# Three chained layers on one core: issue order written out for all engines, and seven products for the second product of two passes

## The chip, the cores and the metric

The kernel runs on one core of one Trainium2 chip. The metric is device time in microseconds, as the median of several executions. The engines that matter are PE (TensorE, matrix products), DVE (VectorE), ACT (ScalarE), POOL (GpSimd) and SP, whose queue issues the DMA transfers.

## The reference

Four batches of attention between 512 tokens and 32 state vectors (8 heads of 64) give 4 x (512 + 32) = 2176 rows of 512. These rows go through two layers:

```
scores = x @ state.T / 8;   xread = softmax(scores) @ state
scores2 = state @ x.T / 8;  sread = softmax(scores2) @ x
h = rows @ w_in             # 512 -> 1024
solu = h * softmax(h);  ln = (solu - mean) / sqrt(var + 1e-6) * g_ln
y = ln @ w_out              # 1024 -> 512
h = y @ w2_in               # 512 -> 2048
g = h * tanh(softplus(h))   # Mish
out = g @ w2_out            # 2048 -> 512
```

The four weight matrices arrive as 64-bit floats, all else as 32-bit.

## The kernel before

**Numbers.** A product that has to be exact to 32 bits is made of three products of shorter ones: each operand is split into a high part (a copy on ACT that rounds, `hi`) and the rest (a subtraction on DVE, `lo`), and PE adds hi*lo, hi*hi and lo*hi into one accumulator in PSUM. A 64-bit weight is first turned into 32 bits by `narrow` (lines 43 to 64): scale the high word (ACT, line 53, or DVE, line 51), shift the low word (ACT, line 55, or DVE, line 57), and either a copy of the sign to 16 bits on ACT (line 59) and one DVE operation (line 60) or two DVE operations (lines 60 and 63).

**First stage (to about 240 us).** The 2176 rows are 17 tiles of 128 rows. Attention and w_in are folded together: state @ w_in is made for each batch (`sw`, tiles swh and swl), and `stage_a0` (line 549) multiplies the softmax weights of a tile (aThi, aTlo) by it, 12 matmuls of 512 columns for each of 16 tiles, and 16 of line 555 for the tile of state rows. `stage_a1` to `stage_a3` (lines 564 to 588) make the softmax and the norm on DVE and ACT; `stage_c` and `stage_e` turn the tile, in part through DRAM (td). `stage_d` (line 645) multiplies by g*w_out in blocks of two tiles (256 columns, the last block 384), 24 matmuls for each of four parts. The result stays in SBUF, features on the partitions (raw_a, raw_c, raw_d).

**Second stage (from about 240 us).** The 17 tiles go in three passes of 6, 6 and 5 tiles; each pass runs over 8 groups (`fp`) of 256 of the 2048 features. In a group the first product (`hp`, line 787, in `group`) is done as a 2 x 2 block product by seven products instead of eight (Strassen's method in Winograd's form); the seven products have 6 matmuls each, of 384 columns in passes 0 and 1 and 320 in pass 2. Seven DVE additions (line 808) and a copy (line 823) put the blocks together, ACT makes Mish of each block twice (lines 817 and 818), once rounded to `gh`, and DVE subtracts for `gl` (line 819). The second product (`po`, `out_parts`, lines 768 to 770) then takes 3 matmuls of 512 columns for each of 2 features blocks and each tile: 36 a group in passes 0 and 1, 30 in pass 2, into one PSUM bank for each tile.

**Weights of the second stage.** In pass 0 they are prepared group by group: `load64` loads 512 KB (tile w, three buffers), narrows it, `pieces_in` makes the four sums that the seven products need and splits seven blocks (lines 188 to 199), and writes them to DRAM (`kept`); `pieces_out` splits w2_out into w2oh and w2ol (lines 217 and 218), which stay in SBUF. Passes 1 and 2 fetch the seven blocks of w2_in again.

**Order.** The text PLAN lists the steps of the first stage, each a whole function (load, narrow, one stage of one tile), and one digit per place that says which engine takes an operation. The second stage is a fixed loop: after each of the seven products comes a part of the `po` work of the group before. A scheduler of the language may move instructions within that.

## Time and profile before

| | |
|---|---|
| median of 3 executions | 606.2 us (603.38 to 608.51) |
| span of the profiled execution | 600.7 us |
| PE busy | 571.1 us, 95% |
| DVE busy | 401.9 us, 67% |
| ACT busy | 302.5 us, 50% |
| DMA | 94.29 MB, mean 157 GB/s |

The profile comes from one execution, whose span runs from its first to its last instruction. The views used are busy time by window, the chain of work that ended last in order of time, the waits (who waited for whom), and timelines of single engines. In a timeline the distance from one start to the next on an engine that never idles is what one instruction occupies; the recorded length of an instruction can be more, since records of neighbours overlap.

### The profile page before, as it was taken

What the parts mean: (1) busy time and instruction counts of PE and PEld (TensorE: products, weight loads), DVE (VectorE), ACT (ScalarE), POOL (GpSimd) and SP (SyncE); (2) the same over time, 40 slices, a digit from 0 to 9 for tenths busy, and PEclk for the clock granted to TensorE, in tenths of its full rate; (3) what the DMA queues carried; (4) which work ended last, traced back from release to release, by engine and by line L of the source; (5) the groups of instructions that cost most, each with busy time, mean ns of one, the idle gap of its engine ahead of it and who ended that gap; (6) DMA issues with size and microseconds to landing.
All of it is one profiled execution on the core that took longest, in us unless ns stands there. A gap on an engine that the chain in (4) does not pass through costs nothing.

```text
span 600.7 us, 8857 instructions
## 1 busy us (share of the span) xinstructions
PE 571.1 (95%) x3371; PEld 491.2 (82%) x3371; DVE 401.9 (67%) x739; ACT 302.5 (50%) x572; POOL 33.4 (6%) x102
## 2 busy tenths in 40 slices
PE   8487899899999999999999999999999999999997
PEld 4145488599799999899989899999999989989885
DVE  3999986898969987878888986333333553443332
ACT  2796866665645644656664765222222452332323
POOL 0002221022111100000000000000000000000000
PEclk9786999899999999999999999999999999999999
DMA  8931321622525645833763575323232354244402
GB/s 321 415 131 35 106 71 52 206 97 71 193 72 172 207 151 195 317 113 144 278 245 117 175 271 210 141 106 140 106 140 106 141 198 153 105 167 163 161 1 88
DMA packets 31050, 94.29 MB, mean 157 GB/s; under 512 B 3616, under 2 KB 11424, under 8 KB 30496
## 3 DMA queue, kind: packets, MB, share of 16 engines
q1 hardware_dynamic: 31008, 93.73, 43.8%
q8 instruction: 26, 0.43, 0.3%
q14 instruction: 16, 0.13, 0.1%
HBM read 69.87 MB, written 23.86 MB: 156 GB/s over the span
## 4 chain that ended last, share of the span: by engine, by line
PE 75%; DVE 13%; DMA 5%; ACT 4%; issue 2%; SPq 1%; ACTq 0%; DVEq 0%
PE hp L787 23%; PE pm L645 16%; PE po L768 8%; PE po L769 8%; PE po L770 8%; PE ph L549 7%; DMA w<-in_w2o 3%; PE ph L555 1%; DVE w L60 1%; DMA xT_t<-in_xT 1%; DVE gw_lo L530 1%; PE tr L603 1%; DMA w<-in_w2i 1%; ACT w L59 1%; DVE wo L60 1%
## 5 line engine op out<-in xcount | busy, mean ns | idle before, releaser
L817 ACT ACTIVATE gh<-c 128x384 fp32r<-128x384 f32 (+1 forms) x96 | 48.9, 509 | 157.5 <-DVE c L808 156.4
L768 PE MATMUL po<-w2ol,gh 128*128 128x512 f32 x272 | 106.8, 393 | 0.1
L769 PE MATMUL po<-w2oh,gh 128*128 128x512 f32 x272 | 106.5, 392 | 0.0
L787 PE MATMUL hp<-xo,w2r 128*128 128x384 f32 (+1 forms) x504 | 93.6, 329 | 0.0
L787 PEld LDWEIGHTS hp<-xo,w2r 128*128 128x128 f32 x504 | 86.5, 188 | 4.8
L787 PE MATMUL hp<-xo,w2swh 128*128 128x384 f32 (+1 forms) x336 | 82.9, 330 | 2.4 <-DVE c L808 2.0
L770 PE MATMUL po<-w2oh,gl 128*128 128x512 f32 x272 | 82.1, 391 | 0.0
L645 PE MATMUL pm<-ln_lo,gw_hi 128*128 128x256 f32 (+1 forms) x256 | 75.3, 294 | 0.0
L645 PE MATMUL pm<-ln_hi,gw_hi 128*128 128x256 f32 (+1 forms) x256 | 75.0, 293 | 0.0
L645 PE MATMUL pm<-ln_hi,gw_lo 128*128 128x256 f32 (+1 forms) x256 | 74.5, 291 | 0.0
L787 PEld LDWEIGHTS hp<-xo,w2swh 128*128 128x128 f32 x336 | 60.5, 188 | 8.3 <-DVE c L808 2.6
L768 PEld LDWEIGHTS po<-w2ol,gh 128*128 128x128 f32 x272 | 51.1, 188 | 9.3 <-ACT gh L817 0.8
L769 PEld LDWEIGHTS po<-w2oh,gh 128*128 128x128 f32 x272 | 51.1, 188 | 8.2
L770 PEld LDWEIGHTS po<-w2oh,gl 128*128 128x128 f32 x272 | 50.1, 188 | 7.7
L787 PE MATMUL hp<-xo,w2swl 128*128 128x384 f32 (+1 forms) x168 | 55.1, 329 | 0.0
L808 DVE TENSOR_TENSOR c<-hp,u 128x384 f32<-128x384 f32 (+1 forms) x48 | 25.6, 534 | 42.7 <-PE hp L787 42.7
L808 DVE TENSOR_TENSOR c<-hp,m 128x384 f32<-128x384 f32 (+1 forms) x48 | 25.6, 532 | 37.3 <-PE hp L787 37.2
L645 PEld LDWEIGHTS pm<-ln_lo,gw_hi 128*128 128x128 f32 x256 | 48.2, 188 | 0.7 <-ACT e L427 0.2
L645 PEld LDWEIGHTS pm<-ln_hi,gw_lo 128*128 128x128 f32 x256 | 48.7, 190 | 0.1
L645 PEld LDWEIGHTS pm<-ln_hi,gw_hi 128*128 128x128 f32 x256 | 48.2, 188 | 0.2
L787 PEld LDWEIGHTS hp<-xo,w2swl 128*128 128x128 f32 x168 | 31.5, 188 | 0.0
L808 DVE TENSOR_TENSOR u<-hp,u 128x384 f32<-128x384 f32 (+1 forms) x24 | 12.8, 535 | 24.7 <-PE hp L787 24.7
(365 smaller groups left out, 907.4 us busy)
## 6 DMA issues: line engine op xcount, KB each, us to landing
w<-in_w2i SPq DMA_DIRECT2D x16, 512.0 KB, 6.5
w<-in_w2o SPq DMA_DIRECT2D x16, 512.0 KB, 4.0
td<-tt SPq DMA_DIRECT2D x9, 512.0 KB, 2.8
ln_lo<-td SPq DMA_DIRECT2D x36, 128.0 KB, 2.9
wi<-in_w_in SPq DMA_DIRECT2D x8, 512.0 KB, 9.1
xT_t<-in_xT SPq DMA_DIRECT2D x16, 256.0 KB, 4.5
wo<-in_w_out SPq DMA_DIRECT2D x4, 1024.0 KB, 11.8
xn_t<-in_xn SPq DMA_DIRECT2D x16, 256.0 KB, 3.8
```

The lines of the kernel that those rows point to most:

```text
L59: nc.scalar.copy(out=src.bitcast(F16)[..., 1], in_=f32(high))
L60: nc.vector.scalar_tensor_tensor(out=words(dst) if sign_on_scalar else low, in0=high, scalar=3, in1=low, op0=ALU.logical_shift_left, op1=A ...
L530: nc.vector.scalar_tensor_tensor(out=gw_lo[sl], in0=wr[:, k, :], scalar=g_k, in1=f32(gw_hi[sl]), op0=ALU.mult, op1=ALU.subtract)
L549: nc.tensor.matmul(out=ph[:, hf * 512:(hf + 1) * 512], lhsT=a_[:, c * P:(c + 1) * P], rhs=w_[:, q, hf * 512:(hf + 1) * 512], start=n == 0, ...
L555: nc.tensor.matmul(out=ph[:, hf * 512:(hf + 1) * 512], lhsT=tl["xs"][:, p, :], rhs=w_in_half[2 * p + hf], start=p == 0, stop=p == 3)
L645: nc.tensor.matmul(out=pm[:, :n], lhsT=w_[:, k, m * P:(m + 1) * P], rhs=l_[:, c0:c0 + 4 * len(blk), k, :], start=cnt == 0, stop=cnt == 23)
L768: nc.tensor.matmul(out=po[ps, j], lhsT=gh[:, c], rhs=wl, start=first, stop=False)
L769: nc.tensor.matmul(out=po[ps, j], lhsT=gh[:, c], rhs=wh, start=False, stop=False)
L770: nc.tensor.matmul(out=po[ps, j], lhsT=gl[:, c], rhs=wh, start=False, stop=f == NF - 1)
L787: nc.tensor.matmul(out=r, lhsT=w_[:, 0, k * P:(k + 1) * P], rhs=x_[:, k, :n], start=cnt == 0, stop=cnt == 6 * len(terms) - 1)
L808: nc.vector.tensor_tensor(out=r, in0=y, in1=x, op=ALU.add)
L817: nc.scalar.activation(out=gh, in_=src, func=AF.Mish)
```

## The change

**Order.** PLAN goes. Every step of both stages is now a generator that issues a few instructions and stops, and ORDER lists 3142 turns of 1019 steps, two letters a turn. Under `manual_schedule` all engines and SP get their instructions in just this order. FLAGS again says which engine takes which operation; the sign copy on ACT (T) is taken at 18 of 28 places, where it was at 4.

**Room layout.** The even and odd batches swap rooms, loads of w2_out have rooms of their own (`s_load64`), and the first loads are three of the four parts of w_out.

**First batch first, in the order of tiles.** Ahead of the first `s_d` (the new `stage_d`) stand all of batch 0's `s_a0` (four tiles), the narrowing of w_in and w_out, and no tile of the other batches.

**Seven products for the second product.** In passes 1 and 2 the weights stand still and the activations move, so the result has features on the partitions, and it is written so (the host puts the rows back). It is a 2 x 2 block product by seven products: 7 blocks x 2 parts x 3 matmuls of 384 (pass 1) or 320 columns (pass 2) a group. Its sums of activations are made in each group (`s_tsum`, `s_tsplit`); five of the seven blocks are added up in SBUF by DVE (`s_block`), two stay in PSUM. The last group of pass 2 stays plain (`s_end`, 8 parts x 6 matmuls of 320). In pass 0 the sums of w2_out are made, split and written to DRAM as well (`s_sums64`, `s_split_osum`, `s_keep_out`), and passes 1 and 2 fetch 14 blocks of 128 KB more a group (`s_fetch_out`). In the first product, sums that DVE made are now made by PE in the PSUM bank (`STEPS`, `s_hp`): five additions and a copy are left.

```diff
-PLAN = """
...
-wm,22 lb,0 lw,3,0 lb,1 lw,1,0 lx,0 lw,1,1 lo,0,1 lw,3,1 lw,0,1 wi,3,1 lw,2,1 lw,0,0 lw,2,0 wi,1,0 lo,1,1 wi,3,0
...
-        for step in PLAN.split():
+FLAGS = dict(
...
+    T="1111100010011000101111011111",
...
+ORDER = (
+    "AAAAA4A4ADA2A2A6A6ABABAEAEAwAwAGAGAkAkA5A5AuAuADA5A5AIAIA3A3BABBA3AKAKA7A3AqAqAsAsBHA7BBBEA7BAAFAFAxAmAmAxAxBEAx"
...
+    live = {}
+    with tc.manual_schedule():
+        for i in range(0, len(ORDER), 2):
+            n = 64 * CODE.index(ORDER[i]) + CODE.index(ORDER[i + 1])
+            if n not in live:
+                step, step_args = steps[n]
+                live[n] = step(*step_args)
+            next(live[n], None)
...
-            for _ in range(1 if b in (B11, T3) else 2):
-                next(more, None)
-            m1_ = temp("m1")
-            nc.scalar.copy(out=m1_, in_=step(A11, B11))
-            active(add("c0", m1_, step(A12, B21)), 0, 0)
-            next(part)()
-            u2 = add("u2", m1_, step(S2, T2))
...
+    def s_load64(which, f):
+        if which and 4 <= f < 8:
+            room = once("room", lambda: x2p.tile([P, 3, 512, 2], U32, tag="x0", name="room"))[:, f % 3]
+        elif which and f >= 8:
+            room = aTp.tile([P, 512, 2], U32, tag="aT", name="w64")
+        else:
+            room = w64_p.tile([P, 512, 2], U32, tag="w64", name="w64")
+        w64[which, f] = room
+        nc.sync.dma_start(out=room, in_=(w2i, w2o)[which][f])
+        yield
+        yield from narrow(nc, f32(room[..., 0]), room, 12 + f)
...
+    def s_split_osum(fp, j):
+        e = f32(w64[1, 2 * fp + j][..., 1]).rearrange("p (n c) -> p n c", c=256)
+        hi, lo = (out_sums(fp, d)[:, 2 * j:2 * j + 2] for d in range(2))
+        nc.scalar.copy(out=hi, in_=e)
+        yield
+        on('H', 4 * fp + 2 + j).tensor_tensor(out=lo, in0=e, in1=f32(hi), op=ALU.subtract)
...
+    def s_keep_out(fp, d, j):
+        if j == 2:
+            nc.sync.dma_start(out=kept_o[fp][:, d, 4:8], in_=f32(out_sums(fp, d)))
+        else:
+            n = 1 if j == 0 and fp < NFP - 1 else 2
+            nc.sync.dma_start(out=kept_o[fp][:, d, 2 * j:2 * j + n], in_=f32(operands(out_place(fp)[d], 2 * j, n)))
+        yield
...
+    def s_fetch_out(ps, fp, d):
+        n = (ps * NFP + fp) % 2
+        t = once(("fo", ps, fp), lambda: [rings[0].tile([P, 8, 256], F32R, tag=f"o{n}{h}", name="w2o" + h) for h in "hl"])
+        W["s", ps, fp] = t
+        if ps == NPASS - 1 and fp == NFP - 1:
+            cuts = ((0, 4),)
+        else:
+            cuts = ((0, 1), (2, 8))
...
+    STEPS = ((A11, B11), (S2, T2), (A12, B21), (S3, T3), (S1, T1), (A22, T4), (S4, B22))
+    WHICH = ((OA11, "b11"), (OA12, "b21"), (OS4, "b22"), (OS1, "t1"), (OS2, "t2"), (OS3, "t3"), (OA22, "t4"))
+    HELD = (5, 6)
...
+    def s_hp(ps, fp):
+        n = width(ps)
+        for s, (a, b) in enumerate(STEPS):
+            t = "xyxyxyx"[s]
+            fresh = s in (0, 1, 4)
+            if fresh:
+                bank[ps, fp, t] = phase2["g"].tile([P, 512], F32, tag="h" + t, name="hp")[:, :n]
+                if s == 4:
+                    bank[ps, fp, "z"] = bank[ps, fp, t]
+            r = bank[ps, fp, t]
+            bank[ps, fp, s] = r
+            x = xop[ps, b]
+            wh, wl = (operands(place, a) for place in W[ps, fp])
+            cnt = 0
+            for k in range(2):
+                for w_, x_ in ((wh, x[1]), (wh, x[0]), (wl, x[0])):
+                    nc.tensor.matmul(out=r, lhsT=w_[:, 0, k * P:(k + 1) * P], rhs=x_[:, k, :n],
+                                     start=s in (0, 1, 3, 4) and cnt == 0, stop=cnt == 5,
+                                     skip_group_check=s not in (0, 1, 3, 4))
+                    cnt += 1
+            yield
...
+        u2 = temp(ps, "u2")
+        nc.vector.tensor_tensor(out=u2, in0=bank[ps, fp, 1], in1=m1_, op=ALU.add)
+        yield
+        u3 = temp(ps, "u3")
+        nc.vector.tensor_tensor(out=u3, in0=bank[ps, fp, 3], in1=u2, op=ALU.add)
+        yield
+        for s, name, u, blk in ((4, "c2", u3, (1, 1)), (5, "c1", u2, (1, 0)), (6, "c0", u2, (0, 1))):
+            c = temp(ps, name)
+            tmp[ps, fp, blk] = c
+            nc.vector.tensor_tensor(out=c, in0=bank[ps, fp, s], in1=u, op=ALU.add)
+            yield
...
+            gh, gl = (phase2["wk"].tile([P, 384], F32R, tag=f"g{j}{half}{t}", name="g" + t, bufs=2)[:, :n] for t in "hl")
+            gs[ps, fp, j, half] = (gh, gl)
+            name = {(0, 0): "b11", (1, 0): "b21", (1, 1): "b22"}.get((j, half))
+            tq[ps, fp, name] = (gh, gl)
+            nc.scalar.activation(out=gh, in_=src, func=AF.Mish)
+            yield
+            value()
+            yield
+            on('L', (ps * NFP + fp) * 4 + 2 * j + half).tensor_tensor(out=gl, in0=vals[ps, fp, j, half], in1=f32(gh), op=ALU.subtract)
+        else:
...
+            t[name] = tsum[ps, fp, name] = phase2["t"].tile([P, 384], F32, tag=name, name=name)[:, :n]
+            y = t[y] if y in t else vals[(ps, fp) + y]
+            on('J', ((ps - 1) * NFP + fp) * 4 + int(name[1]) - 1).tensor_tensor(out=t[name], in0=vals[(ps, fp) + x], in1=y, op=ALU.subtract)
+            yield
...
+        tq[ps, fp, name] = (hi, lo)
+        nc.scalar.copy(out=hi, in_=src)
+        yield
+        on('V', ((ps - 1) * NFP + fp) * 4 + int(name[1]) - 1).tensor_tensor(out=lo, in0=src, in1=f32(hi), op=ALU.subtract)
...
+        held = i in HELD
+        tag = f"po{2 * HELD.index(i) + m}" if held else f"po{4 + m}"
+        if first or not held:
+            po[ps, i, m] = phase2["o"].tile([P, 512], F32, tag=tag, name="po")[:, :n]
+        r = po[ps, i, m]
+        c = slice(m * P, m * P + P)
+        nc.tensor.matmul(out=r, lhsT=wh[:, a, c], rhs=x[1], start=first or not held, stop=False)
+        nc.tensor.matmul(out=r, lhsT=wh[:, a, c], rhs=x[0], start=False, stop=False)
+        nc.tensor.matmul(out=r, lhsT=wl[:, a, c], rhs=x[0], start=False, stop=last or not held)
+        yield
+        side = on('E', ps - 1)
...
+            if not held:
+                add(s[i], r, s[i])
...
+            for w_, x_ in ((wh, gl), (wh, gh), (wl, gh)):
+                nc.tensor.matmul(out=r, lhsT=w_[:, a, c], rhs=x_, start=cnt == 0, stop=cnt == 5)
+                cnt += 1
```

## Rows read from the trace of the kernel before

**Rows 1.** Windows: length, busy us of PE, PEld, DVE, ACT, POOL; clock, DMA share, GB/s

```profile
0.00:84.00 84.00, 62.96 (x369) 35.81 (x369) 71.36 (x124) 56.81 (x98) 9.76 (x37) 0.86 0.49 180
84.00:240.00 156.00, 153.97 (x1192) 136.94 (x1193) 129.85 (x211) 92.44 (x161) 23.64 (x66) 0.99 0.43 142
240.00:361.00 121.00, 118.97 (x592) 107.10 (x593) 103.18 (x214) 73.95 (x144) 0.00 (x0) 1.00 0.57 207
361.00:486.00 125.00, 125.00 (x625) 113.26 (x624) 54.66 (x102) 42.04 (x88) 0.00 (x0) 1.00 0.36 131
486.00:595.00 109.00, 108.97 (x595) 97.44 (x594) 42.89 (x93) 36.08 (x85) 0.00 (x0) 1.00 0.36 132
```

**Rows 2.** The start: windows, line 645's first matmul (PE timeline), line 549 until then (window)

```profile
20.00:40.00 20.00, 11.77 (x42) 3.94 (x42) 20.00 (x32) 17.56 (x25) 0.00 (x0) 0.72 0.72 277
40.00:60.00 20.00, 15.69 (x69) 11.54 (x62) 19.48 (x38) 13.37 (x28) 3.58 (x12) 0.68 0.18 53
...
83.94 0.39 PE L645 MATMUL pm<-ln_lo,gw_hi 128*128 128x256 f32 x1
...
0.00:83.90 83.90, 21.31 (x72) 14.85 (x72) 0.86 0.49 181
```

**Rows 3.** Chain in time order: start, us, engine, tile, line, count

```profile
177.91 5.46 PE ph L549 x24
...
347.87 1.37 PE po L770 x6
...
411.13 1.06 PE hp L787 x6
...
426.78 1.06 PE hp L787 x6
...
515.46 0.88 PE hp L787 x6
```

**Rows 4.** DVE timeline, passes 0 and 2: start, us, line, operation, tiles

```profile
312.99 0.55 DVE L808 TENSOR_TENSOR c<-hp,m 128x384 f32<-128x384 f32 x1
313.46 0.69 DVE L60 SCALAR_TENSOR_TENSOR w<-w 128x512 uint32<-128x512 uint32 x1
314.06 0.56 DVE L819 TENSOR_TENSOR gl<-a__3249,gh 128x384 fp32r<-128x384 f32 x1
...
590.01 0.48 DVE L808 TENSOR_TENSOR m<-hp,u 128x320 f32<-128x320 f32 x1
590.41 0.48 DVE L819 TENSOR_TENSOR gl<-a__5792,gh 128x320 fp32r<-128x320 f32 x1
```

**Rows 5.** ACT timeline, pass 0

```profile
297.25 0.51 ACT L818 ACTIVATE a__3100<-c 128x384 f32<-128x384 f32 x1
297.67 1.34 ACT L59 CAST w<-w 128x512 f16<-128x512 f32 x1
298.76 0.73 ACT L53 ACTIVATE w<-w 128x512 f32<-128x512 f32 x1
...
303.40 1.21 ACT L198 CAST w2r<-w 128x512 fp32r<-128x512 f32 x2
```

**Rows 6.** Waits: engine, tile, line, releaser; us in total, times, longest

```profile
ACT w L55 <- DMA w<-in_w2i: 7.5, 4, 2.3
...
ACT w L55 <- DMA w<-in_w2o: 5.6, 3, 2.4
...
ACT w L53 <- DMA w<-in_w2o: 3.1, 2, 2.5
...
ACT w L53 <- DMA w<-in_w2i: 2.9, 3, 1.2
```

**Rows 7.** Last matmul and last copy, timeline of all engines

```profile
595.84 0.39 PE L770 MATMUL po<-w2oh,gl 128*128 128x512 f32 x1
...
597.02 0.59 ACT L736 COPY ob<-po 128x512 f32<-128x512 f32 x1 [0.62 <-DMA out<-ob]
```

More of the change, by code (lines that the diff above doesn't have):

```diff
@@ L1 @@
 import math
-from contextlib import ExitStack, contextmanager
-from itertools import chain
+from contextlib import ExitStack
 import concourse.bass as bass
@@ L137, in how, with once @@
-    def how(i):
-        return eng('B', i, False, True)
-    def signs(i):
-        return eng('T', i, False, True)
-    def keep_up(dst, n):
-        for _ in range(n):
-            nc.tensor.matmul(out=dst, lhsT=spare[:, :dst.shape[0]], rhs=spare.unsqueeze(1).to_broadcast([P, 4, P]),
-                             start=True, stop=True)
-    def times(i):
-        return 3 * int(flags["D"][i])
+    tl, raw = {}, {}
+    def once(key, make):
+        if key not in tl:
+            tl[key] = make()
+        return tl[key]
@@ new lines, in w_in_half, with s_warm, s_load_bd @@
+    def w_in_half(i):
+        if i == 7:
+            return once("w_in_7", lambda: m1.tile([P, 512], F32, tag="w7", name="w_in_7"))
+        return once("w_in", lambda: wx_p.tile([P, 7, 512], F32, tag="wx7", name="w_in_t"))[:, i]
+    def s_warm(n):
+        dst = ps_m.tile([P, 512], F32, tag="mm", name="warm")
+        for _ in range(n):
+            nc.tensor.matmul(out=dst, lhsT=spare, rhs=spare.unsqueeze(1).to_broadcast([P, 4, P]), start=True, stop=True)
+        yield
+    def s_load_bd(i):
+        dst, src = ((bd_t, bd), (st_t, stT))[i]
+        nc.sync.dma_start(out=dst, in_=src)
+        yield
@@ new lines, in s_tok_turn, with s_scores0 @@
+    def s_tok_turn(b, q):
+        ex = toks[b].rearrange("p (c q r) n -> p c q (r n)", c=4, q=2)
+        tr = turn4(ex[:, :, q, :]).rearrange("p c t -> p (c t)")
+        yield
+        yield from weights_of(b, q, tr)
+    def s_scores0(q):
+        sts[0, q] = st = ps_m.tile([P, S], F32, tag="mm", name="st")
+        for j in range(2):
+            p = 2 * q + j
+            nc.tensor.matmul(out=st[of_head(j), :], lhsT=bd_t[:, p, :], rhs=xT_t[0, p], start=True, stop=True)
+            yield
@@ L161, in ring, with operands, ring_in @@
+    def operands(place, i, n=1):
+        for i0, n0, t in place:
+            if i0 <= i and i + n <= i0 + n0:
+                return t[:, i - i0:i - i0 + n]
+    def ring_in(fp):
         if fp % 2 == 0:
@@ L895 @@
     r = run_bass_kernel_spmd(nc, [arrays], core_ids=[0])
-    return r.results[0]["out_0"]
+    flat = r.results[0]["out_0"]
+    y = np.empty((NTOK, DM), flat.dtype)
+    done = 0
+    for ps, places in enumerate(PASSES):
+        n = len(places) * P
+        part = flat[done * DM:(done + n) * DM]
+        part = part.reshape(n, DM) if ps == 0 else part.reshape(DM, n).T
+        done += n
+        for j, place in enumerate(places):
+            t = TILE_AT[place]
+            rows = part[j * P:(j + 1) * P]
+            if t < 16:
+                b, s = divmod(t, 4)
+                y[b * (S + NS) + s * P:][:P] = rows
+            else:
+                for b in range(B):
+                    y[b * (S + NS) + S:][:NS] = rows[b * NS:(b + 1) * NS]
+    return y
```

1400 lines of the change are left out of this document (779 added, 621 removed).

## Prediction

> **What bounds the kernel now.** I read the windows by stage first [rows 1]. Up to 84 us PE is busy 63 of 84 us at a mean clock of 0.86 of full, while DVE is busy 71. After that PE is the bound: its idle time is 2.0 us from 84 to 240, 2.0 us in pass 0 (240 to 361), and none in passes 1 and 2. So only two things can move the end: fewer or shorter matmuls after about 84 us, or an earlier time at which PE has enough to do. The windows of the start show why PE waits: from 20 to 60 us DVE is busy 39.5 of 40 us, PE 27.5, and the clock granted to PE is 0.72 and 0.68 of full, a mean over stretches at its two levels of 1.2 and 2.4 GHz [rows 2]. The first matmul of line 645 starts at 83.9 us; by then 72 of the 192 matmuls of line 549, six tiles of sixteen, are done [rows 2]. The end hangs on PE: the last matmul ends at 595.84 + 0.39 = 596.2 us, then a copy and a store take the 4.5 us to 600.7 [rows 7].
>
> The chain in time order gives PE's prices [rows 3]: six `hp` matmuls of 384 columns follow each other in 1.06 us (177 ns each), of 320 columns in 0.88 us (147 ns); six of 512 take 1.37 us (229 ns); a tile of line 549 takes 5.46 / 2 = 2.7 us. A group of pass 1 lasts 426.78 - 411.13 = 15.65 us = 42 x 0.177 + 36 x 0.229: no gap.
>
> The DVE timeline gives starts in an unbroken run [rows 4]: an operation of 384 columns begins 0.47 us before the next, one of 512 0.60, one of 320 0.40, though their records are 0.55, 0.69 and 0.48 long. On ACT [rows 5] a Mish of 384 occupies 0.42 us, the sign copy 298.76 - 297.67 = 1.09, a copy of 512 0.6.
>
> **Part 1, the second product: PE loses 11.2 us.** Pass 0 keeps 36 matmuls of 229 ns a group. Pass 1: 7 blocks x 2 parts x 3 = 42 matmuls of 384 columns, 42 x 0.177 = 7.43 us in place of 36 x 0.229 = 8.24: 0.81 x 8 groups = 6.5 us. Pass 2: 42 x 0.147 = 6.17 in place of 30 x 0.229 = 6.87: 0.70 x 7 groups = 4.9 us; the plain last group has 48 x 0.147 = 7.06, 0.2 more. Together 6.5 + 4.9 - 0.2 = 11.2 us. Shape and count of `hp` stay.
>
> What pays for it is DVE. A group of passes 1 and 2 has 5 additions after `hp`, 3 `gl`, 4 sums, 4 splits and 10 block additions, 26 where there were 11. At the distance between starts that is 26 x 0.47 = 12.2 us in a group of 7.43 + 42 x 0.177 = 14.9 us of PE (82%) in pass 1, and 26 x 0.40 = 10.4 of 12.3 us (84%) in pass 2; it was 55 of 125 and 43 of 109 us [rows 1]. ACT has 12 operations, some 5 us. I cost this work at nothing, covered by PE, but allow 2 us over both passes for places where a bank waits for DVE: five of seven blocks use only two banks, and each must be read by DVE before PE may refill it. Without cover it costs what DVE exceeds PE by (rival 2).
>
> Whether a DVE operation blocks the next for 0.47 us or for its whole record of 0.55 is what this rests on, and [rows 4] show 0.47 where nothing waited. The Trainium skill, "VectorE: DVE Perf Modes", section "The DRAIN you can't avoid", says that the next operation cannot issue until the pipe of the one before is empty, and advises fewer operations above all; it speaks against this part. Taken as the whole record, pass 2 would need 26 x 0.48 = 12.5 us of DVE for 12.3 of PE, and the end would come some 1.5 us later; the row bears out the shorter figure.
>
> **Part 2, the start: 13.6 us earlier at the first `s_d`.** In ORDER, what stands on DVE ahead of the first `s_d` is 20 operations of 1024 columns (1.13 each, going on from 0.47 and 0.60), 46 of 512 (0.60) and some 24 scalar or tiny ones (7 us, an estimate): 22.6 + 27.6 + 7 = 57 to 58 us. Before it was 71.4 [rows 1]: two tiles fewer are in work and five of the second narrowing operations of w_in and w_out have become sign copies on ACT. DVE's time not busy before 83.9 us was 83.9 - 71.3 = 12.6 us. With the same 12.6 the first `s_d` comes at 57.7 + 12.6 = 70.3. Bounds: 66.7 if only the 9 us until the first data are lost, 83.9 if nothing is gained. I take 70.3, not less, because ACT's list for the same stretch is 56 us too (it was 56.8 of 84 us), so two engines are full that wait for each other. PE's own list ahead of it is some 36 us and fits at either clock. The clock of 0.7 stays until then.
>
> What PE has not done by then: two more tiles of line 549 (4 of 16 done instead of 6), 5.5 us, and some 2 us of small products: 7.5 us.
>
> **Part 3, pass 0: 4 us lost.** Here the change adds: sums, splits and stores of w2_out. The list between the first `hp` of pass 0 and that of pass 1 has PE 117 us (56 products and 84 of the 96 x 3 `po` matmuls), DVE 111 and ACT 104. Before, DVE was busy 103 and ACT 74 of 121 us [rows 1]; ACT's 30 us more are mostly 19 sign copies of 1.09 us and 12 copies for the sums. DMA moved 207 GB/s x 121 us = 25 MB at a share of 0.57; six groups of 14 blocks of 128 KB add 11 MB: share 0.82. The waits in which ACT stood for a load in pass 0 are 7.5 + 5.6 + 3.1 + 2.9 = 19.1 us in 12 times, 1.6 us each [rows 6]; they cost PE little because ACT had slack of 121 - 74 = 47 us. Now ACT has 13. Behind a narrowing operation that waits stand on ACT the Mish of the group, and behind that PE, whose `hp` banks it must read. With the same 19.1 us of waits 19.1 - 13 = 6 us reach PE, 4 more than the 2.0 idle now. SP's order counts too: stores of a split stand ahead of the loads of a later group, so a late split makes a load late. Bounds: 0 if the new rooms make loads early enough, 20 if each of the 22 loads of this stretch waits 1.6 us (35 - 13 - 2).
>
> **Part 4, no cost or gain.** Host order of rows, output stores and the fetch of 1.8 MB more a group (131 to about 250 GB/s, share 0.36 to 0.7, each fetch a group ahead) are hidden. The tail of 4.5 us stays: copy or addition, then store.
>
> **Sum.** 70.3 + (596.2 - 83.9 = 512.3) - 11.2 + 7.5 = 578.9; + 4 in pass 0 + 2 in passes 1 and 2 = 584.9; + 4.5 = 589.4 us of span, against 600.7. The median of the runs, 606.2, lies 5.5 above the profiled span, so 594.9: **595 us**, 1.8% less. Without any loss and with the best start: 589.4 - 6 - 3.6 = 580, 585 on the median's scale.
>
> **Rivals.**
> 1. *Pass 0 becomes the bound.* Loads wait as often as there are loads: 20 us in place of 4, and 611; half of it, 603. For it: PE, DVE and ACT are at 117, 111 and 104, and nothing catches up. Against it: w2_out has rooms of its own, so its loads are issued some 8 us ahead.
> 2. *DVE becomes the bound in passes 1 and 2* (slower). It decides from 14.9 / 26 = 0.57 us an operation in pass 1 and 12.3 / 26 = 0.47 in pass 2. At the whole record plus 0.05 us for a wait: 26 x 0.60 = 15.6 and 26 x 0.53 = 13.8, + 0.7 x 8 + 1.5 x 7 = 16, and with chains that reach through ACT (Mish, sum, split, block) somewhat more: 611 to 620. For it: the order is fixed, so one late operand holds all of DVE. Against it: [rows 4].
> 3. *The start gains nothing*: the change doesn't do there what it says. ACT and DVE wait for each other, and the first `s_d` stays at 83.9: + 13.6, 608.
>
> **How the numbers follow.** A measurement of this kernel can tell about 1% from no change: under 600 is faster, over 612 slower. The forecast, 589 to 601, has 0.50; a better one, 580 to 589, 0.14; rival 1 (601 to 611) 0.16; rival 3 (about 608) 0.09; rival 2 and above 0.11. So faster 0.62, same 0.26, slower 0.12. The range 584 to 609 leaves out the best corner and rival 2; the forecast's own is 589 to 601.
>
> **What will show it.** Right: groups of pass 1 14.9 us apart and of pass 2 12.3, with no idle PE; DVE busy near 85% there; the first `pm` matmul near 70 us; pass 0 some 6 us longer than its matmuls. Wrong: `hp` or the block matmuls waiting for DVE in passes 1 and 2 (rival 2), ACT waiting for w2_in loads with PE idle behind it (rival 1), or a first `pm` near 84 (rival 3).

## The result, and the profile after

The changed kernel takes **597.4 us** (median of 6 executions, 595.56 to 598.95); the kernel before, executed beside it, 603.8 us (6 executions, 601.18 to 608.51). The ratio is 0.990, 95% interval 0.986 to 0.994: 1.0% faster. Measured once more beside the later experiments it was 0.989 (0.984 to 0.994). The profiled execution has a span of 596.8 us against 600.7, and its own time was 598.6: 1.8 us lie around the span. The spans of the six executions run from 593.8 to 597.2 us.

| | before | after |
|---|---|---|
| profiled span | 600.7 us | 596.8 us |
| first `s_d` (`stage_d`) matmul | 83.9 us | 68.7 us |
| last matmul of the first stage ends, about | 239.5 us | 232.4 us |
| first `hp` of pass 1 | 360.9 us | 362.2 us |
| first `hp` of pass 2 | 486.1 us | 479.9 us |
| last matmul ends | 596.2 us | 593.0 us |
| DVE busy | 401.9 us | 503.2 us |
| ACT busy | 302.5 us | 362.6 us |
| DMA | 94.3 MB | 136.1 MB |

The same windows as [rows 1], cut at the changed kernel's own landmarks (length, busy us of PE, PEld, DVE, ACT, POOL; granted clock, DMA share, GB/s):

```profile
0.00:68.70 68.70, 57.30 (x345) 31.72 (x345) 58.16 (x92) 55.45 (x81) 11.33 (x38) 0.85 0.63 236
68.70:232.40 163.70, 159.05 (x1204) 141.43 (x1204) 130.48 (x205) 97.75 (x165) 19.97 (x69) 0.98 0.38 129
232.40:362.20 129.80, 122.63 (x589) 107.91 (x589) 118.08 (x247) 112.38 (x201) 0.00 (x0) 0.97 0.82 302
362.20:479.90 117.70, 117.70 (x662) 115.05 (x662) 96.06 (x188) 53.67 (x112) 0.00 (x0) 1.00 0.73 257
479.90:593.00 113.10, 110.89 (x727) 107.60 (x726) 99.60 (x221) 43.33 (x105) 22.43 (x22) 1.00 0.72 255
```

The reader is to see three things. The start is over 15 us earlier than before. Pass 1 shrank from 125 to 118 us, and PE has no idle time in it. But pass 0 grew from 121 to 130 us, with 7.2 us of idle PE where [rows 1] have 2.0, and the first stage behind the start has 4.7 where it had 2.0. In all, PE stands idle for 4.7 + 7.2 + 2.2 = 14 us from 68.7 us on (before: 4 us from 84 us on).

The busy column hides short waits, since a matmul's record (0.31 to 0.34 us at the full clock) is about twice the distance to the next one (0.147 to 0.177). Counted by the prices of [rows 3], pass 0 has 336 `hp` and 252 `po` matmuls, 336 x 0.177 + 252 x 0.229 = 117.2 us, and takes 129.8: 12.6 us more. Pass 1 shows nothing of the kind. Pass 2's window has 677 matmuls of 320 columns and 48 of 384, 108.0 us, and takes 113.1: 5.1 us more, where the column shows 2.2. Before, pass 0 and pass 2 took some 2.6 and 1.1 us more than their matmuls.

The clock takes more. The next windows are two short stretches, the second of them just behind the first group of pass 0:

```profile
199.40:206.20 6.80, 5.62 (x27) 5.33 (x26) 5.11 (x11) 5.31 (x8) 0.00 (x0) 0.50 0.80 241
232.40:236.90 4.50, 2.26 (x13) 1.94 (x12) 3.71 (x9) 3.46 (x6) 0.00 (x0) 1.00 0.40 144
236.90:243.70 6.80, 5.61 (x18) 5.62 (x19) 3.41 (x6) 3.87 (x7) 0.00 (x0) 0.50 0.94 317
```

The granted clock is 0.50, that is 1.2 GHz, in both stretches of 6.8 us. PE was busy 5.6 us in each; at the full clock this work takes about half: some 2.8 us lost twice. Idle and slow time together are 14 + 5.6 = 19.6 us; before, 4 us of idle and some 1.6 us lost to the low clock (0.99 over 156 us, [rows 1]). So by these columns PE loses 14 us more than before, where the prediction had 6.

What stands ahead of the second stretch shows on PE and ACT (start, us, engine, line, operation, tiles; in brackets the idle time before it and its releaser):

```profile
234.32 0.34 PE L855 MATMUL hp<-xo,w2swl 128*128 128x384 f32 x1
238.09 1.01 PE L855 MATMUL hp<-xo,w2swh 128*128 128x384 f32 x2 [3.43 <-ACT m L866]
...
239.21 0.84 PE L855 MATMUL hp<-xo,w2swh 128*128 128x384 f32 x2
...
240.17 0.84 PE L855 MATMUL hp<-xo,w2swh 128*128 128x384 f32 x2
```

```profile
229.71 0.69 ACT L150 ACTIVATE w<-w 128x512 f32<-128x512 f32 x1 [2.68 <-DMA w<-in_w2i]
231.89 0.43 ACT L676 CAST w2r<-w 128x256 fp32r<-128x256 f32 x1 [1.49 <-DVE w L164]
233.41 1.24 ACT L676 CAST w2r<-w 128x512 fp32r<-128x512 f32 x2 [1.09 <-DVE w L652]
234.54 0.69 ACT L153 ACTIVATE w<-w 128x512 uint32<-128x512 uint32 x1
235.26 1.35 ACT L158 CAST w<-w 128x512 f16<-128x512 f32 x1
...
237.53 0.50 ACT L866 COPY m<-hp 128x384 f32<-128x384 f32 x1
```

PE's third product needs the copy `m` of the first, which could start at about 233.8 us. ACT makes it at 237.5: it had stood 2.7 us for a load of w2_in, 1.5 and 1.1 us for DVE's part of the same weights, and all of that, the sign copy of 1.1 us with it, stood ahead of `m` in its list. Then the clock is low: three `hp` matmuls take 240.17 - 239.21 = 0.96 us, where [rows 3] have 1.06 for six. The waits of the stretch from 180 to 365 us (engine, tile, line, releaser; us in total, times, longest) name the same chain:

```profile
PE hp L855 <- ACT m L866: 3.7, 2, 3.4
PE pm L611 <- ACT raw_d L616: 3.1, 2, 1.9
...
ACT w L150 <- DMA w<-in_w2i: 8.7, 6, 2.7
...
ACT w L150 <- DMA w<-in_w2o: 4.4, 4, 1.9
...
DVE w L155 <- DMA w<-in_w2i: 3.9, 2, 2.2
```

### The profile page after: what moved, and what is told of

Its sections match the earlier page's. It is cut to its first block, busy times and chain, and to the rows that moved or that the text cites. A ratio compares the mean times of both kernels' runs of the same rounds, so it can differ in the third digit from the quotient of the medians.

```text
span 596.8 us, 9744 instructions
## 1 busy us (share of the span) xinstructions
PE 567.6 (95%) x3521; PEld 503.7 (84%) x3521; DVE 503.2 (84%) x949; ACT 362.6 (61%) x662; POOL 53.7 (9%) x129
## 5 line engine op out<-in xcount | busy, mean ns | idle before, releaser
L611 PE MATMUL pm<-ln_l,gw_hi 128*128 128x256 f32 (+1 forms) x256 | 77.3, 302 | 3.1 <-ACT raw_d L616 3.1
L611 PE MATMUL pm<-ln_h,gw_hi 128*128 128x256 f32 (+1 forms) x256 | 76.0, 297 | 0.0
L611 PE MATMUL pm<-ln_h,gw_lo 128*128 128x256 f32 (+1 forms) x256 | 75.6, 295 | 0.0
L967 DVE TENSOR_TENSOR acc<-po,acc 128x384 f32<-128x384 f32 (+1 forms) x136 | 68.6, 522 | 4.4 <-PE po L962 4.0
L611 PEld LDWEIGHTS pm<-ln_l,gw_hi 128*128 128x128 f32 x256 | 49.4, 193 | 6.6 <-ACT raw_d L616 3.6
L611 PEld LDWEIGHTS pm<-ln_h,gw_hi 128*128 128x128 f32 x256 | 49.4, 193 | 0.7
L611 PEld LDWEIGHTS pm<-ln_h,gw_lo 128*128 128x128 f32 x256 | 49.8, 194 | 0.0
L877 DVE TENSOR_TENSOR c<-hp,u 128x384 f32<-128x384 f32 (+1 forms) x72 | 38.4, 533 | 12.3 <-PE hp L855 11.7
L525 PE MATMUL ph<-swh,aT 128*128 128x512 f32 x128 | 40.0, 404 | 1.5 <-DVE swl L483 0.8
L960 PE MATMUL po<-ql,w2oh 128*128 128x384 f32 (+1 forms) x120 | 39.9, 333 | 1.1 <-DVE acc L967 1.0
L962 PE MATMUL po<-qh,w2ol 128*128 128x384 f32 (+1 forms) x120 | 38.8, 323 | 0.0
```

The source lines that it names most:

```text
L525: nc.tensor.matmul(out=ph[:, hf * 512:(hf + 1) * 512], lhsT=a_[:, c * P:(c + 1) * P], rhs=w_[:, q, hf * 512:(hf + 1) * 512], start=q == 0 ...
L611: nc.tensor.matmul(out=pm[:, :n], lhsT=w_[:, k, m * P:(m + 1) * P], rhs=l_[:, c0:c0 + 4 * len(blk), k, :], start=k == 0 and j == 0, stop=k ...
L877: nc.vector.tensor_tensor(out=c, in0=bank[ps, fp, s], in1=u, op=ALU.add)
L960: nc.tensor.matmul(out=r, lhsT=wh[:, a, c], rhs=x[1], start=first or not held, stop=False)
L962: nc.tensor.matmul(out=r, lhsT=wl[:, a, c], rhs=x[0], start=False, stop=last or not held)
L967: on.tensor_tensor(out=o, in0=x, in1=y, op=ALU.add)
```

## The experiments

**The theory.** What PE loses from 190 to 340 us comes from transfers: the stores of split weights that Part 3 adds fill the DMA engines (share 0.82 in pass 0, [rows 1] had 0.57), loads of the next weights land late, ACT or DVE stands for one in its fixed order, and an operation that PE needs stands behind. **The rival:** DVE (118 us busy of 130) and ACT (112) are simply full, and any order would lose as much. Beside this pair the runs measure each part alone: the seven products, DVE's room in passes 1 and 2, POOL's share, the start. Times of one group of runs are compared by their ratio to the kernel before on the same chip; the changed kernel is at 0.990 (0.986 to 0.994). Groups of `hp` are written (pass, group).

### Fewer loads, fewer stores

```diff
+        elif which == 0 and f:
...
         w64[which, f] = room
-        nc.sync.dma_start(out=room, in_=(w2i, w2o)[which][f])
+        if which or f == 0:
+            nc.sync.dma_start(out=room, in_=(w2i, w2o)[which][f])
```

> All loads of w2_in but the first are left out (the narrowing, sums, splits and stores run on what the room holds, so the weights are not the right ones); ORDER and every other instruction stay. In the changed kernel the stretch from the second group of pass 0 to the first of pass 1 (248.3 to 362.2 us) lasts 113.9 us, of which PE loses some 7, and before it PE stands 3.4 us for m. Theory A, the waits of ACT and DVE for these loads (12.6 us) are what PE loses: the 3.4 us shrink to under 1, the second group starts near 243, the stretch takes 109 to 110.5 us, and the time is 589 to 592. Theory B, DVE (118 busy of 130 us) and ACT (112) are simply full: the stretch stays at 113 to 114 us and the time within 2 us of the changed kernel.

```diff
     def s_keep_out(fp, d, j):
+        if fp:
+            return
...
-            nc.sync.dma_start(out=f32(t[d])[:, i:e], in_=kept_o[fp][:, d, i:e])
+            nc.sync.dma_start(out=f32(t[d])[:, i:e], in_=kept_o[0][:, d, i:e])
```

> The engines' work stays, but the stores of w2_out's blocks to DRAM are left out for all groups but the first (12 MB less, passes 1 and 2 fetch the first group's blocks, so their products are not the right ones). Theory C, the transfers delay each other: at 262 to 282 us the DMA share was 1.03, and without these stores the loads land in 5 us instead of up to 8: ACT's waits for loads halve, and the stretch from 248 to 362 us takes 110 to 111.5 us. Theory A in its other form, the loads are issued late because their rooms come free late, or theory B: the stretch stays at 113 to 114 us.

Without the loads (each narrowing of w2_in then works in a room that another load has filled; the lines behind the first dots choose it): 590.4 us, ratio 0.982 (0.978 to 0.986), span 588.2. Without the stores: 592.0 us, 0.985 (0.981 to 0.988), span 590.2. Each has two executions only. The stretch from group (0,1) to group (1,0) as a window, first of the changed kernel, then without the loads, then without the stores:

```profile
248.30:362.20 113.90, 110.20 (x537) 96.55 (x538) 106.81 (x224) 101.50 (x184) 0.00 (x0) 1.00 0.83 307
```

```profile
243.40:353.50 110.10, 109.20 (x537) 96.84 (x538) 106.47 (x224) 101.12 (x184) 0.00 (x0) 1.00 0.75 275
```

```profile
244.30:354.60 110.30, 109.25 (x537) 96.84 (x538) 106.41 (x224) 101.50 (x184) 0.00 (x0) 1.00 0.63 218
```

DVE and ACT do the same work in all three (106 to 107 and 101 us, 224 and 184 instructions), and PE's idle time falls from 3.7 to about 1 us. The group (0,1) starts 4 to 5 us earlier as well, and the low clock at 237 us does not appear in either. So the engines are not too full for 110 us. Taking away 12 MB of stores shortens the stretch as much as taking away the loads of w2_in. The load that ACT stood 2.7 us for at 229.71 us shows how. SP issues it at nearly the same time in both runs (first the changed kernel, with the stores ahead of it, then without the stores, with ACT's operation on the loaded weights):

```profile
218.78 4.62 SPq L728 DMA_DIRECT2D ko<-w2o  x3
223.67 0.33 SPq L635 DMA_DIRECT2D w<-in_w2i  x1
```

```profile
223.87 1.06 SPq L635 DMA_DIRECT2D w<-in_w2i  x2
...
227.36 0.69 ACT L150 ACTIVATE w<-w 128x512 f32<-128x512 f32 x1
```

With the stores it lands 6.0 us after its issue, without them by 227.36 us, after 3.5 us at most, and ACT doesn't wait. ACT's and DVE's waits for loads of w2 from 180 to 365 us fall from 20.0 to 10.9 us. The price of these stores is 3 us by the ratios (the intervals, 0.986 to 0.994 and 0.981 to 0.988, overlap) and 6.6 by the two spans. Most of the latter may be the clock: counted as (1 - granted clock) x PE busy in windows of 2 us, PE lost 5.6 us to the low clock in the profile of the changed kernel and nothing in that without the stores.

### Less work at the same bytes

```diff
     def s_sums64(which, fp):
+        if which == 1:
+            return
...
     def s_split_osum(fp, j):
+        return
+        yield
...
-            nc.sync.dma_start(out=kept_o[fp][:, d, 4:8], in_=f32(out_sums(fp, d)))
+            pass
...
+            nc.sync.dma_start(out=kept_o[fp][:, d, 4 + 2 * j:6 + 2 * j], in_=f32(operands(out_place(fp)[d], 2 * j, 2)))
```

> The sums of w2_out and their splits are left out in pass 0 (per group 4 additions of 256 and 2 subtractions of 512 on DVE, 2 copies of 512 on ACT); in their place the plain blocks are stored, the same bytes, so the products of passes 1 and 2 are not the right ones. Without the stores the stretch from the second group of pass 0 to the first of pass 1 took 110.3 us, without the loads of w2_in 110.1, against 113.9. Theory B, full engines: 6 groups x (2.5 us of DVE and 1.1 of ACT) = 15 and 7 us less work shorten it to 108 to 110.5 us as well. Theory A, only late transfers count and the work was hidden: 112.5 to 114 us.

Slower, which neither theory had: 606.1 us (600.7 to 609.5), ratio 1.005 (1.000 to 1.009). The stretch took 122 us although DVE and ACT had less to do in it (93 and 96 us busy):

```profile
249.70:371.70 122.00, 114.21 (x537) 100.07 (x538) 92.79 (x188) 95.61 (x172) 0.00 (x0) 0.96 0.80 287
```

The edit stores the second half of the blocks beside the first, so more stores stand together ahead of a load. On SP's queue and on ACT one such place reads (L732 and L733 are stores, L635 the load):

```profile
326.76 0.41 SPq L684 DMA_DIRECT2D ki<-w2r  x1
327.26 0.47 SPq L732 DMA_DIRECT2D ko<-w2ol  x1
327.78 1.18 SPq L733 DMA_DIRECT2D ko<-w2ol  x1
329.05 1.02 SPq L635 DMA_DIRECT2D w<-in_w2i  x1
...
335.69 0.67 ACT L150 ACTIVATE w<-w 128x512 f32<-128x512 f32 x1 [4.83 <-DMA w<-in_w2i]
```

```profile
325.00:330.00 5.00, 5.00 (x27) 4.56 (x27) 4.47 (x10) 4.97 (x7) 0.00 (x0) 1.00 1.04 393
330.00:335.00 5.00, 5.00 (x26) 4.51 (x25) 3.45 (x8) 0.86 (x2) 0.00 (x0) 1.00 0.99 313
335.00:340.00 5.00, 2.54 (x13) 1.77 (x11) 1.13 (x2) 4.31 (x8) 0.00 (x0) 1.00 0.10 41
340.00:345.00 5.00, 4.30 (x13) 3.59 (x13) 4.76 (x11) 4.27 (x11) 0.00 (x0) 0.56 0.76 215
```

Eight stores of 256 KB and one of `ki` go out from 323.6 us on, the load at 329.05, and it lands 6.6 us later. ACT stands 4.8 us, PE is busy for half of the next 5 us, and then the clock falls (0.56). ACT's waits for loads of w2 in the stretch from 180 to 365 us rose to 28.9 us (13.5 in the changed kernel). The rival as stated, full engines that lose as much in any order, is refuted by the two runs above; here 14 us less of DVE work did not even help, because the loads came later still. At this place the transfers that stand ahead of the load decide. The run's own reading as "same bytes" was too simple: the place of the stores was changed too.

Full engines are half of the account all the same. The kernel before had more of these waits, not fewer: 19.1 us on ACT ([rows 6], all of them between 180 and 365 us) against 13.5, and 24.7 against 20.0 with DVE's added. PE idled 2.0 us in pass 0 with them. There ACT was busy 74 of 121 us and DVE 103; now it is 112 and 118 of 130. A late load costs PE where the engine that stands for it has no time left to catch up.

### Order alone: copies first, more of it, loads first

ORDER, with its turns written as step(arguments).turn; the first of three such edits:

```diff
 d(5,2).2
+d(5,3).1
+d(5,2).3
+d(5,2).4
 load64(1,0).3
...
-d(5,2).3
...
-d(5,2).4
...
-load64(0,4).2
...
-load64(0,4).3
...
 hp(0,0).0
-x_split(0,2).0
 hp(0,0).1
 post(0,0).0
...
 act(0,0,0,0).1
...
+act(0,0,0,0).2
+x_split(0,2).0
...
+load64(0,4).2
 post(0,0).2
+load64(0,4).3
```

> Same work, same order on PE and of the transfers; only on ACT and DVE three copies out of PSUM (of two s_d parts at 198 to 202 us, and m of the first group of pass 0 at 237 us) and the two Mish behind the last are put ahead of narrowing operations that wait for a load. Theory A, the copies are late because ACT works in order behind an operation that waits for a load: PE's waits of 1.9, 1.2 and 3.4 us go, and where the clock fell to 1.2 GHz after them (199 to 206 and 237 to 244 us, 6 us lost) it may stay: the second group of pass 0 starts near 242 instead of 248.3 us and the end comes 4 to 6 us earlier, 591 to 593.5 us. Theory B, the loads set the pace whatever stands ahead: the wait goes to the next operation that needs the narrowed weights, and the time falls by 1 us or less, 596.5 to 598.

597.9 us, ratio 0.992 (0.990 to 0.995): no gain. In the profile the edit did at its place what theory A says; the windows that were at 0.50 are at full clock, PE's first group is free of its 3.4 us, and group (0,1) starts at 244.9 instead of 248.3:

```profile
199.40:206.20 6.80, 3.24 (x28) 3.03 (x27) 5.22 (x11) 4.80 (x7) 0.00 (x0) 1.00 0.73 231
232.40:236.90 4.50, 4.38 (x25) 3.82 (x24) 3.10 (x8) 4.25 (x8) 0.00 (x0) 1.00 0.59 177
236.90:243.70 6.80, 5.72 (x28) 4.59 (x27) 5.95 (x12) 6.13 (x8) 0.00 (x0) 1.00 0.96 345
```

But new waits stand behind: 3.6 us for `ln_l` (transposes of the last tile) from 202 us on, which eat what the other two copies gained and behind which the clock falls again (0.66 from 205 to 210 us), and 2.1 us for `c` at 242.8. Of the 3.4 us at group (0,1), 1.7 are left at group (1,0). The next run took these waits too:

```diff
 sums64(1,0).0
+turn(14,0).2
...
 split_out(0,0).1
+turn(14,1).2
...
-turn(14,0).2
...
-turn(14,1).2
...
 hp(0,0).5
+post(0,0).4
...
 hp(0,1).0
+post(0,1).0
 load64(1,5).1
```

> The same work; ORDER alone is changed in seven places, so that an operation that PE waits for stands ahead of one that waits for a load on the same engine: the copies as in the run that put copies first, and also the two splits of tile 14 that the transposes of tile 16 then waited 3.6 us for, the additions c of the first and third group of pass 0 (PE waited 2.1 and 1.5 us for them), and m of the second group (0.8). Theory A, each of these waits was only a matter of place: of some 8 us of PE's waits between 196 and 276 us 5 or more go, the third group of pass 0 starts near 254 to 256 instead of 261.8 us, and the time is 0.7 to 1% below that of the changed kernel on this chip. Theory B, the loads set the pace: each wait moves to the next operation behind, and the time is within 0.4% of the changed kernel.

In the same group of runs the changed kernel was measured again:

> The changed kernel once more, beside the others of this group, so that they can be compared on one chip: 0.985 to 0.994 of the kernel before, as in its first measurement (0.9896).

Both take 596.4 us (the second order 0.992, 0.988 to 0.995; the changed kernel 0.989, 0.984 to 0.994). Theory B: PE's waits from 196 to 276 us are 6.9 us, where the first profile of the changed kernel has 6.5 and the second 6.4; only their places change (the view of waits of the second order):

```profile
PE pm L611 <- ACT raw_d L616: 4.6, 2, 2.3
PE po L912 <- DVE gl L900: 1.9, 1, 1.9
```

The third edit of ORDER leaves the engines' lists and moves transfers on SP:

```diff
-keep_out(6,0,1).0
...
-keep_out(6,1,1).0
...
-keep_out(6,0,0).0
...
-keep_in(5,0).1
...
-keep_out(6,1,0).0
...
 load64(0,14).0
+keep_out(6,0,1).0
...
+keep_out(6,1,1).0
...
+keep_out(6,0,0).0
...
+keep_in(5,0).1
...
+keep_out(6,1,0).0
...
```

> The same work and the same bytes; in ORDER the stores of split weights that stand up to some 26 turns ahead of a load of the second stage's weights are put behind it (all on SP; nothing else moves). Theory A, a load lands late because stores that were issued just before it fill the transfer engines (8 stores of 2 MB ahead of one load made it land after 6.6 us where ACT then stood 4.8 us): ACT's and DVE's waits for loads from 180 to 365 us fall from 19 to 12 us or less, the second group of pass 0 starts 2 to 4 us earlier, the stretch from it to the first group of pass 1 takes 111 to 113 instead of 113.9 us, and the time is 0.5 to 1% below the changed kernel, 0.979 to 0.985 of the kernel before. Theory B, the loads are late since their rooms come free late, and the stores now wait behind them: waits and time stay, 0.987 to 0.995. A loss is possible too, where stores that come later meet the next loads: above 0.995.

595.5 us, ratio 0.990 (0.986 to 0.994): the time of the changed kernel. Waits of ACT and DVE for loads fell from 20 to 13 us, and until 275 us it paid: group (0,1) starts at 243.6, and the two groups (0,1) and (0,2) have no idle PE (the first window). The second window gives it back:

```profile
243.60:275.60 32.00, 31.91 (x156) 28.21 (x157) 31.55 (x67) 31.41 (x55) 0.00 (x0) 1.00 0.75 282
275.60:359.00 83.40, 78.66 (x383) 70.13 (x382) 75.16 (x158) 70.30 (x131) 0.00 (x0) 0.98 0.86 318
```

PE idles 4.7 us in these 83, 3.1 of them in one wait for the second Mish of a block (L889); the same stretch of the changed kernel, 282.1 to 362.2, idles 2.1. ACT shows the old pattern at a new place, the Mish behind a wait for a load:

```profile
286.05 0.67 ACT L150 ACTIVATE w<-w 128x512 f32<-128x512 f32 x1 [3.03 <-DMA w<-in_w2o]
...
288.07 0.47 ACT L889 ACTIVATE a__3083<-hp 128x384 f32<-128x384 f32 x1
```

The stores that were moved meet later loads; that this is what made this load late was not shown. None of the three orders beats the changed kernel.

### The stores on a queue of their own

```diff
-            nc.sync.dma_start(out=kept_o[fp][:, d, 4:8], in_=f32(out_sums(fp, d)))
+            nc.gpsimd.dma_start(out=kept_o[fp][:, d, 4:8], in_=f32(out_sums(fp, d)))
...
-            nc.sync.dma_start(out=kept_i[fp][:, d, i:i + n], in_=f32(w))
+            nc.gpsimd.dma_start(out=kept_i[fp][:, d, i:i + n], in_=f32(w))
```

> The stores of split weights to DRAM (26 MB in the late first stage and pass 0) are issued by POOL on its own queue instead of SP; bytes, places and all else stay. Theory C1, the loads stand behind the stores in one queue: they land 2 to 3 us sooner, ACT's and DVE's waits for loads (18.8 us from 180 to 365 us) halve, and the time falls by 3 to 4 us (0.5 to 0.7%). Theory C2, it is the bytes, whatever the queue: nothing within 0.3%. Theory C3, POOL's issuing disturbs DVE, as POOL's additions did at 492 us: the time rises by 3 us or more.

599.1 us, ratio 0.995 (0.992 to 0.998), beside 0.989 (0.984 to 0.994) of the changed kernel: 2.7 us slower by the medians, though the intervals touch. The loads do not land sooner: the median from issue to landing of a w2_in load is 5.9 us (5.4 with the stores on SP), ACT's waits for these loads rose from 8.7 to 11.9 us (all waits of ACT and DVE for loads of w2: 18.9 against 20.0), and PE's wait for `m` from 3.7 to 5.4. Theory C1 is out: it isn't the one queue. The page "DMA: Bandwidth & Descriptors" of the Trainium skill, section "Issuing engines are not separate DMA queues", says that transfers from every issuing engine run interleaved on the same 16 DMA engines, and that another queue saves only the time to issue; this run agrees. Whether POOL's issuing also disturbed DVE can't be read apart here: DVE's busy time in the stretch is the same (105.6 and 106.8 us).

### The parts of the change alone

Seven products undone in pass 1 (the core of the edit):

```diff
     def s_block(ps, fp, i, m):
+        if ps == 1:
...
+                po_plain(fp, f, j)
...
     def s_tsum(ps, fp):
+        if ps == 1:
+            return
...
+        nc.tensor.matmul(out=po["q", j], lhsT=gh[:, c], rhs=wl, start=k == 1, stop=False)
+        nc.tensor.matmul(out=po["q", j], lhsT=gh[:, c], rhs=wh, start=False, stop=False)
+        nc.tensor.matmul(out=po["q", j], lhsT=gl[:, c], rhs=wh, start=False, stop=k == NF)
```

> The second product of pass 1 alone is done plainly again: 36 matmuls of 512 columns a group into six banks, no sums, no additions in SBUF; pass 2 keeps its seven products. Theory A, the seven products pay in full: a group of pass 1 goes from 14.7 back to 15.6 us, 7 us more in eight groups, less up to 2 us of PE's waits at the change from pass 1 to pass 2, which go with the additions: 602 to 604 us on the scale of 597.4. Theory B, waits for DVE eat the gain of pass 1: 597 to 599.

606.9 us, ratio 1.007 (1.004 to 1.010). The stretch of pass 1, plain; with the seven products it is the window from 362.20 to 479.90 us in the section on the result:

```profile
361.70:486.60 124.90, 124.90 (x626) 113.24 (x624) 46.07 (x83) 39.44 (x82) 0.00 (x0) 1.00 0.54 192
```

Theory A: 7.2 us in the stretch (6.4 by the spans, some 10 by the ratios; by the count above, the profile of this run lost 1.7 us to the low clock, that of the changed kernel 5.6). DVE's 50 us more of work are hidden in full. Without this part in pass 1 the changed kernel would not be faster than the kernel before.

DVE's room in passes 1 and 2:

```diff
             nc.vector.tensor_tensor(out=c, in0=bank[ps, fp, s], in1=u, op=ALU.add)
+            if ps:
+                nc.vector.tensor_tensor(out=temp(ps, "m1"), in0=c, in1=c, op=ALU.add)
             yield
```

> Three more DVE additions of 384 (pass 2: 320) columns in every group of passes 1 and 2, into a tile that nobody needs; the result stays. Theory A, an operation occupies DVE for the distance of starts (0.47 and 0.40 us): 29 x 0.47 = 13.6 of the 14.7 us of a group of pass 1 and 29 x 0.40 = 11.6 of 12.35 us of pass 2; PE stays without gaps but for 1 to 2 us at the changes of pass: 598 to 600 us. Theory B, it occupies DVE for its whole record (0.55 and 0.48): 16.0 and 13.9 us, 1.3 x 8 + 1.55 x 7 = 21 us more, 618 us.

612.1 us, ratio 1.016 (1.013 to 1.019), some 16 us more: neither theory by its own reason. DVE's timeline of this run:

```profile
422.72 0.55 DVE L928 TENSOR_TENSOR t<-a__4527,a__4456 128x384 f32<-128x384 f32 x1
423.30 0.56 DVE L928 TENSOR_TENSOR t<-a__4489,t 128x384 f32<-128x384 f32 x1
423.78 0.55 DVE L969 TENSOR_TENSOR acc<-po,acc 128x384 f32<-128x384 f32 x1
424.24 0.55 DVE L928 TENSOR_TENSOR t<-a__4489,a__4527 128x384 f32<-128x384 f32 x1
...
433.18 0.56 DVE L877 TENSOR_TENSOR c<-hp,u 128x384 f32<-128x384 f32 x1
433.77 0.56 DVE L879 TENSOR_TENSOR m<-c 128x384 f32<-128x384 f32 x1
```

An operation begins 0.47 us after the one before it, as in [rows 4], but 0.58 or 0.59 where it reads what that one has just written (`t` at 423.30, `m` at 433.77). The three additions read the `c` just ahead of them, so they cost 3 x 0.59 = 1.8 us. With the one sum that reads the sum just ahead of it, four of the 29 operations are of this kind: about 29 x 0.47 + 4 x 0.12 = 14.1 us, an estimate, beside PE's 84 x 0.177 = 14.9 us of matmuls. At that load DVE is the bound here and there, though it is never full: the waits of PE from 405 to 486 us, 2.1 us, are all for DVE, and three groups in the middle of pass 1 take 47.8 us instead of 45.0, 15.9 each instead of 15.0. So the cover of Part 1 ends within 1.8 us a group; the prediction's 82% left less room than it looked.

POOL's share:

```diff
-    E="11",
+    E="00",
...
-    J="0000000000000000000000000000100000000000000000000000000000000000",
+    J="0000000000000000000000000000000000000000000000000000000000000000",
```

> The 22 additions and subtractions that POOL has in the changed kernel (10 block additions at the end of pass 1, 10 at the end of pass 2, one sum of activations, one gl) go to DVE. Theory A, POOL slows DVE while both work: between 480 and 506 us of the changed kernel two DVE subtractions lasted 1.31 and 1.12 us where the others take 0.48, while POOL was at work, and PE lost 3.5 us there; then DVE's stretched operations return to 0.48 and 0.55, the 11 more operations of 0.47 find room, and 2 to 3 us of PE's gaps at 494 to 502 us go: 594.5 to 595.5 us on the scale of 597.4. Theory B, POOL relieves DVE: DVE gets about 5 us more in each of the two places, PE's gap grows from 3.5 to 6 us or more, and the time rises to 600 to 603.

(The one `gl` on POOL moved as well, in L.) 599.2 us, ratio 0.994 (0.992 to 0.997): about 3 us slower, the direction of theory B, though the interval touches that of the changed kernel. The idle time of PE in pass 2 rose from 2.2 to 3.8 us, less than theory B's 6. The disturbance that theory A starts from is real, and it goes in this run (the two subtractions take 0.48 and 0.49 us); relief is worth more.

The start:

```diff
-    T="1111100010011000101111011111",
+    T="0000000000001000101111011111",
```

> In the narrowing of w_in and w_out the seven sign copies on ACT (1.09 us each) go back to second operations on DVE (0.60 us each): DVE gets 4.2 us more before the first s_d, ACT 7.6 us less. Theory A, DVE sets the start (the prediction's sum, DVE's list plus 12.6 us): the first s_d goes from 68.7 to 72 to 73 us, and the end comes 3 to 4 us later, since PE has no slack behind it. Theory B, ACT sets it: the first s_d comes earlier, 64 to 68 us. Theory C, the start is given back later, where PE waits for the weights of the second stage anyway: the first s_d moves, the first group of pass 0 (232.4 us) by less than half of it.

The first `s_d` goes from 68.7 (67.1 to 68.9 in the profiles with the same start) to 71.2 us; DVE is busy 63.1 us until then instead of 58.2, ACT 44.8 instead of 55.5. The time is 600.3 us, ratio 0.998 (0.996 to 1.000). Theory A in kind: DVE's list sets the start, though 5 us more of it cost 2.5, and the start is not given back later (group (0,0) comes 2.3 us later, the last matmul 2.0; by the ratios it is 5 us, and this profile lost 1.7 us to the low clock, that of the changed kernel 5.6).

## Why the prediction was right, and where it was wrong

The forecast was 595 us, and 597.4 came; the result lies in the range and on the side of faster, by its edge. By its steps:

- **Start: right.** 70.3 us forecast for the first `s_d`, 68.7 measured. DVE was busy 58.2 us until then (57 to 58 forecast). From 20 to 60 us PE was at clocks of 0.76 and 0.94, where [rows 2] have 0.72 and 0.68. Rival 3 is out, and the run with the sign copies back on DVE shows that DVE's list is what counts.
- **Work carried past the start: high.** 7.5 us forecast; 24 more matmuls of 512 columns stand behind the first `s_d` (224 instead of 200), 24 x 0.23 = 5.5 us.
- **Part 1: right.** 7.2 us in pass 1 measured alone, 6.5 forecast; three groups in the middle of pass 1 take 15.0 us each (14.9 forecast), and from 532.6 to 569.5 us three groups of pass 2 take 12.3 us each. PE has no idle time in steady groups. Rival 2 did not come, but its point lies closer than the 82% made it look.
- **Waits in passes 1 and 2: low.** Some 2 us were allowed. The column shows 2.2 us of idle PE, nearly all of it at the change from pass 1 to pass 2 (494 to 502 us), where DVE has two passes' work at once and POOL beside it, and the rest in the last group; but pass 2 takes 5.1 us more than its matmuls, so the term was too low by some 3 us.
- **Pass 0: the step that failed.** 4 us more were forecast, by setting ACT's waits for loads (19 us) against ACT's slack (13 us) as sums; pass 0 was to be "some 6 us longer than its matmuls". It took 129.8 us, 12.6 more than its 117.2. Both sums were off, and their difference is not what PE pays. The 19.1 us of [rows 6] are the waits from 180 us on; in pass 0 itself ACT had 13.0 us of them before and 5.1 after. Set against a slack of 129.8 - 112.4 = 17.4 us that would cost nothing. PE paid because slack in sum doesn't pay for a wait at one place: one wait of 2.7 us, ahead of pass 0, and what followed from it delayed `m` by 3.7 us, with nothing between to take it, and the low clock behind it cost 2.8 more. The direction of the prediction's mechanism (ACT stands for a load, PE behind it) was right, and rival 1 came at about half of its price. What the runs show in place of the sum is that the 12 MB of stores that Part 3 adds make single loads land late (6.0 us instead of 3.5 at most), on engines that are nearly full: without them pass 0 takes 121.9 us. The prediction counted these stores in the DMA share (0.82, as measured) and named their place ahead of the loads, but gave it no price.
- **Not seen at all: the first stage behind the start.** The preparation of the first groups of w2 runs there beside the last tiles, and PE waited for `raw_d` (3.1 us), with a low clock behind it. The sum carried [rows 1]'s 84 to 240 us over as it was. That the stage still took 163.7 us, close to the sum's 155.6 + 7.5 = 163.1, is luck: less work had been carried into it, and 12 `hp` matmuls (2.1 us) that the kernel before makes within it come behind it now.
- **From span to median: an error to the good.** The 5.5 us were the median of three executions less the profiled span. The time around a span is 1.8 us (598.6 - 596.8), so the profiled execution of before stands for some 602.5; the three executions took longer than most, for the medians of the kernel before beside the later runs were 600.8 to 602.2. So the span was missed by 7.4 us (589.4 against 596.8), the median by 2.4. That the median came so near is luck, and the ratio shows it: 1.8% less was forecast, 1.0% came. Of the 7.4 us pass 0 is 6.6 and passes 1 and 2 some 2 to 3; the start and the tail gave 2.3 back.

What stays open: whether another order recovers the 3 to 5 us by the ratios (7 to 9 by the spans) that the runs without stores and without loads show. Three orders moved the waits and not the end. The time that PE loses at 1.2 GHz differs between profiles (5.6 and 4.5 us in the two of the changed kernel, 1.7 with copies first, none without the stores, 1.5 before), and how much of the differences between medians is due to it was not separated. The second half of the start's change, batch 0 first, was not tried alone.

## What to carry to other kernels

A wait for a load is to be priced at its place: what stands behind it on that engine, and how far ahead of its user that is; a sum of waits set against a sum of slack hides the one that PE sees. Stores that nobody waits for are not free where loads land in time only just: look at what stands ahead of each load in the transfer queue, and at how full the engine is that will stand for it. Work in the shadow of PE is free only while its engine keeps some room: here DVE cost PE nothing at 88% busy (39.5 of 45.0 us in the middle of pass 1), and three more operations cost PE about 1 us a group.
